# A planner fed with traced intervals, patient engines, and two blocks' operands of x made during the attention

## The chip, the cores and the metric

The kernel runs on one core of a Trainium2 chip. The metric is the device time of one execution in microseconds (us); three executions of the kernel before gave 893.12, 893.55 and 894.0, median 893.55. Engines are named as in the profile: PE (TensorE matmul), PEld (its weight load), DVE (VectorE), ACT (ScalarE), POOL (GpSimd), SP (the queue from which transfers are issued).

## The reference

```python
# B, H, S, D = 4, 8, 576, 64; window 128; x has 2304 tokens of 512, d_ff 2048
scores = scale * q @ k.T
scores = where(0 <= rel < 128, scores + slope[h] * -abs(rel), -1e9)
attn = softmax(scores)            # exp(s - max) / (sum + 1e-9)
x = attn @ v                      # heads side by side: 2304 x 512
h = x @ w_in;  x = where(h > 0, h, exp(min(h, 0)) - 1) @ w_out     # first layer (ELU)
h = x @ w2_in; x = (h * sigmoid(h)) @ w2_out                       # second layer (SiLU)
```

The two layers' weights come as 64-bit floats and are turned into 32-bit ones on the chip.

## The kernel before

**Work.** The attention has 36 units (9 pairs of 128-token groups x 4 pairs of heads). A unit is: scores on PE (`s`, L454), bias and maximum on DVE (L465), exponential on ACT (L473), inverse of the sums on DVE (L485, L486), scaling on POOL (L492), transposes on PE (`t`, L511), their eviction to `pt` by DVE and ACT (L521, L523); for every two units a product with v on PE (`a`, L543). Each product of the layers is made of three: every fp32 operand is split into a rounded part (ACT) and a remainder (DVE).

**First sweep of layer one.** While the attention runs, the tokens whose x is done (blocks of 256, then four of 512 tokens) go through the first four of the sixteen 128-wide slices of d_ff: `hidden` on PE (L587), ELU on ACT and DVE (L572, L573), `output_first` on PE (L614), into `acc`. One piece is three matmuls. These pieces fill PE between the units' own matmuls. The last block's pieces come behind the attention.

**The other sweeps.** The rest of both layers goes by 768-token blocks b = 0, 1, 2 in steps k = 0 to 14. A step's input products use seven combinations of four quarters of x (tiles `c`, matmuls L873); then come its output products (L964). Step 0 is block 0, step 1 block 1, step 2 block 2, then the order turns. `make(k)` loads x from DRAM (`xs`), forms differences on DVE (L759), rounds on ACT (L769) and takes the remainder on DVE (L734): 22 DVE and 14 ACT instructions per block. For blocks needed again, the seven `c` are stored to DRAM (`d`, L741), and later steps load them back with `reload` (L810). In the kernel before, steps 0, 1 and 2 use `make`; step 0's stands just behind the attention, since the tiles `c` lie where the attention's tiles were (`opened`).

**Order.** `Plan.run` is a list scheduler that runs while the program is built: each instruction has an engine, a cost, what it must follow, and a latest start (`late`) that comes from due times on PE's instructions. Of the instructions whose inputs are there by its clock, an engine takes the one with the smallest `late`. The result is a fixed order on each engine (and on SP); on the chip each engine runs its own order, one behind the other, waiting where it must. A unit's due time is `unit_due(u)`.

## Time and profile before

| what | value |
|---|---|
| median of three executions | 893.55 us (893.12 to 894.0) |
| the profiled execution: its time, its span | 892.67 us, 890.9 us (1.8 us lie outside the span) |
| PE busy | 867.2 us, 97% of the span, 5520 matmuls |
| DVE, ACT, POOL busy | 600.8, 503.1, 132.0 us |
| DMA | 130.98 MB, mean 147 GB/s |

How to read it: the profiled execution's 892.67 us is its span plus 1.8 us. Where a PE timeline says "x12 | 3.06 us", that is the time from the first matmul's start to the last one's modelled end; from the start of one run to the start of the next is the time a run really takes. A busy PE says only that matmuls were under way: at a lower granted clock the same matmuls are busy for longer.

### The profile page before, as it was taken

The page shows a single profiled execution, that of the slowest core. Times are in us where ns is not written, and L with a number is a line of the kernel's source. Part 1 is how long each engine was busy: PE and PEld are TensorE (multiplying, and loading weights), DVE is VectorE, ACT ScalarE, POOL GpSimd, SP SyncE. Part 2 cuts the span into 40 slices and gives each one's busy share as a digit, 9 for nine tenths or more (in the row PEclk, how much of TensorE's full clock was granted, in tenths as well). Part 3 has the DMA queues.
Part 4 walks back from the last instruction along what each step waited for, and adds up shares of the span by engine and source line. Part 5 has one row for each costly group of instructions (what it writes and reads, how often), then busy time and mean ns, then how long its engine had stood idle before and what let it go on. Part 6 is the DMA issues. An engine that isn't in the chain of part 4 may idle for free.

```text
span 890.9 us, 14913 instructions
## 1 busy us (share of the span) xinstructions
PE 867.2 (97%) x5520; PEld 774.6 (87%) x5520; DVE 600.8 (67%) x1385; ACT 503.1 (56%) x1191; POOL 132.0 (15%) x238
## 2 busy tenths in 40 slices
PE   5989999999979999999999999999999999999998
PEld 3667777777979999999999998989899998989997
DVE  6988876639988888896848878564847334634333
ACT  6877776657764747472637557465654244533331
POOL 8653433311010001110000003000101000000000
PEclk9979999999979999999999999999999999999999
DMA  9834341214947102181535567061327060126721
GB/s 312 277 99 149 108 155 55 72 61 164 336 126 283 36 24 72 71 321 46 216 128 216 212 228 268 10 248 48 118 80 286 1 249 24 72 71 213 250 104 71
DMA packets 55928, 130.98 MB, mean 147 GB/s; under 512 B 3760, under 2 KB 35760, under 8 KB 55856
## 3 DMA queue, kind: packets, MB, share of 16 engines
q1 hardware_dynamic: 55712, 129.91, 41.0%
q8 instruction: 43, 0.70, 0.3%
q14 instruction: 29, 0.24, 0.1%
q10 hardware_dynamic: 144, 0.13, 0.0%
HBM read 93.06 MB, written 36.96 MB: 146 GB/s over the span
## 4 chain that ended last, share of the span: by engine, by line
PE 89%; DVE 7%; ACT 2%; POOL 1%; issue 1%; POOLq 0%; DVEq 0%; ACTq 0%
PE m L964 38%; PE m L873 34%; PE m L614 5%; PE m L587 5%; PE a L543 3%; PE s L454 3%; PE t L511 2%; DVE c L734 1%; DVE raw L318 1%; DVE w L295 1%; DVE p L465 1%; DVE raw L320 1%; DVE t L759 0%; DVE e L572 0%; DVE e L573 0%
## 5 line engine op out<-in xcount | busy, mean ns | idle before, releaser
L964 PE MATMUL m<-w,g 128*128 128x512 f32 (+1 forms) x876 | 211.7, 387 | 0.0
L964 PEld LDWEIGHTS m<-w,g 128*128 128x128 f32 x876 | 161.6, 188 | 26.4
L964 PE MATMUL m<-g,w 128*128 128x384 f32 x864 | 165.4, 342 | 4.7 <-DVE h L886 2.8
L964 PEld LDWEIGHTS m<-g,w 128*128 128x128 f32 x864 | 154.9, 192 | 6.3 <-DVE h L886 3.1
L315 POOL TENSOR_SCALAR raw<-raw 128x512 f32<-128x512 f32 x60 | 50.8, 847 | 544.5 <-DMA raw<-in_moe_w_in_dram 233.3
L851 DVE TENSOR_TENSOR g<-e,g 128x384 fp32r<-128x384 f32 x168 | 92.6, 559 | 41.1 <-ACT e L837 39.4
L873 PE MATMUL m<-c,wd 128*128 128x384 f32 x504 | 101.4, 336 | 0.1
L873 PE MATMUL m<-c,wc 128*128 128x384 f32 x504 | 100.8, 336 | 0.0
L873 PE MATMUL m<-c,wa 128*128 128x384 f32 x504 | 99.5, 336 | 1.1 <-DVE c L734 0.6
L886 DVE TENSOR_TENSOR hs<-m,hs 128x384 f32<-128x384 f32 x84 | 46.7, 556 | 76.2 <-PE m L873 75.6
L978 DVE TENSOR_TENSOR acc<-m,acc 128x384 f32<-128x384 f32 (+2 forms) x85 | 51.4, 608 | 67.4 <-PE m L964 66.3
L882 ACT ACTIVATE hs<-m 128x384 f32<-128x384 f32 x84 | 41.2, 490 | 92.2 <-PE m L873 91.8
L873 PEld LDWEIGHTS m<-c,wa 128*128 128x128 f32 x504 | 89.1, 188 | 4.5 <-DVE acc L978 0.9
L873 PEld LDWEIGHTS m<-c,wd 128*128 128x128 f32 x504 | 89.0, 188 | 2.6 <-ACT h L882 0.4
L873 PEld LDWEIGHTS m<-c,wc 128*128 128x128 f32 x504 | 89.2, 188 | 2.2 <-DVE c L734 0.2
L492 POOL TENSOR_SCALAR p<-p,sm 128x192 f32<-128x192 f32 (+1 forms) x144 | 67.0, 484 | 97.2 <-DVE sm L486 58.7
L473 ACT ACTIVATE p<-p,neg 128x192 f32<-128x192 f32 (+1 forms) x144 | 63.0, 442 | 12.6 <-DVE neg L465 12.4
L614 PE MATMUL m<-g,w 128*128 128x512 f32 (+1 forms) x240 | 60.1, 393 | 1.3 <-DVE ex L573 1.0
L587 PE MATMUL m<-x,w 128*128 128x512 f32 (+1 forms) x240 | 58.0, 382 | 0.0
L614 PEld LDWEIGHTS m<-g,w 128*128 128x128 f32 x240 | 42.5, 198 | 13.1 <-issue 2.7
L838 ACT ACTIVATE g<-hs 128x384 fp32r<-128x384 f32 x48 | 25.2, 525 | 46.6 <-DVE hs L886 46.5
L873 PE MATMUL m<-c,wb 128*128 128x384 f32 x252 | 50.6, 336 | 0.0
(119 smaller groups left out, 1185.4 us busy)
## 6 DMA issues: line engine op xcount, KB each, us to landing
c<-d SPq DMA_DIRECT2D x49, 768.0 KB, 6.3
d<-c SPq DMA_DIRECT2D x28, 768.0 KB, 5.2
raw<-in_moe_w_in_dram SPq DMA_DIRECT2D x32, 512.0 KB, 5.3
raw<-in_moe_w_out_dram SPq DMA_DIRECT2D x28, 512.0 KB, 3.6
k<-in_k_dram SPq DMA_DIRECT2D x16, 384.0 KB, 4.6
d<-xs SPq DMA_DIRECT2D x7, 768.0 KB, 3.9
v<-in_v_dram SPq DMA_DIRECT2D x18, 256.0 KB, 2.7
xs<-xd SPq DMA_DIRECT2D x6, 768.0 KB, 4.8
```

What stands on the lines that cost most here:

```text
L315: add("POOL", 0.75, lambda: nc.gpsimd.tensor_scalar(f32(top()), f32(top()), 2.0 ** -112, 1.0, op0=ALU.mult, op1=ALU.mult), w=top_k)
L454: nc.tensor.matmul(T["s", j][x * (P // 2):(x + 1) * (P // 2), e, c0:], T["q", t % 2][rows, hp, o:o + P // 2], T["k", t % 2][rows, hp, o + ...
L473: nc.scalar.activation(dst, dst, AF.Exp, bias=T["neg", u % 5][:, i:i + 1], scale=-1.0, accum_out=T["sm", u % 5][:, e, j:j + 1])
L492: nc.gpsimd.tensor_scalar(dst, dst, T["sm", u % 5][:, e, j:j + 1], 1.0, op0=ALU.mult, op1=ALU.mult)
L587: nc.tensor.matmul(T[m][:, 0:w], a[:, cs], T["x0", b2][:, c, 0:w], start=(c == 0 and x == 0), stop=(c == NKC - 1 and x == 2))
L614: nc.tensor.matmul(T[m][:, 0:w], a[:, cs], b2[:, 0:w], start=(f == 0 and x == 0), stop=(f == FIRST_F - 1 and x == 2))
L851: add("DVE", 0.58, lambda: nc.vector.tensor_tensor(T[gk[1]], T[ek], f32(T[gk[0]]), op=ALU.subtract), r=[ek, gk[0]], w=[gk[1]])
L873: nc.tensor.matmul(T[m][:, 0:HALF], a[:, cs], x[:, j, c, :], start=(begin and c == 0 and n == 0), stop=(c == 1 and n == 2), skip_group_che ...
L882: add("ACT", 0.5, lambda: nc.scalar.activation(T[s], T[m][:, 0:HALF], AF.Copy), r=[m], w=[s])
L886: add("DVE", 0.58, lambda: nc.vector.tensor_tensor(T[s], T[m][:, 0:HALF], T[s], op=ALU.add), r=[m], w=[s])
L964: nc.tensor.matmul(T[m][:, 0:w], l, rr, start=(f == 0 and x == 0), stop=(f == n - 1 and x == 2))
L978: add("DVE", 0.2 + w / 1000.0, lambda: nc.vector.tensor_tensor(dst, T[m][:, 0:w], dst, op=ALU.add), r=[m], w=dk)
```

## The change

There are three parts.

1. **Costs.** Nearly all costs given to the planner become shorter (a 384-column DVE difference 0.57 to 0.475, a bias instruction 0.4 to 0.29, the exponential 0.6 to 0.445). The delay between engines, 0.2 for all, becomes 0.08 plus a drain time of the first engine; it is no longer counted between two instructions of one engine. A transfer's cost becomes 1.6 us and 300 GB/s (from 1.8 and 220). Units fall due every 3.2 us for the first 14, then every 5.0 (from 5.2).
2. **Patience.** ACT, DVE and POOL don't start an instruction where one that is over 3 us more urgent becomes ready before it would end; they take a shorter one or stay idle.
3. **`make_ahead(b)`**, for blocks 0 and 1: the same 22 DVE and 14 ACT instructions as in `make`, but issued during the attention, in the space of the third `acc` tile and two small tiles `st`, with stores of half a `c` (384 KB) to DRAM. Steps 0 and 1 then load their `c` back (7 loads of 768 KB each). x is stored per pair of groups instead of per block, and step 6's operands are stored in halves. `sm` and `neg` have four buffers instead of five.

```diff
-    LINK = 0.2
-    DMA_START = 1.8
-    DMA_RATE = 220.0e3
+    LINK = 0.08
+    DRAIN = {"PE": 0.2, "ACT": 0.1, "DVE": 0.08, "POOL": 0.04}
+    DMA_START = 1.6
+    PATIENT = "ACT", "DVE", "POOL"
+    GAIN = 3.0
+    DMA_RATE = 300.0e3
...
                     x = min(can, key=lambda x: (x[1].late, x[1].n))
+                    if eng in self.PATIENT:
+                        soon = [u for u in queues[eng] if now < u[0] < now + x[1].cost - 0.1 and u[1].late < x[1].late - self.GAIN]
+                        if soon:
+                            at = min(u[0] for u in soon)
+                            can = [x for x in can if now + x[1].cost <= at + 0.1]
+                            if not can:
+                                continue
+                            x = min(can, key=lambda x: (x[1].late, x[1].n))
...
-    UNIT, START = 5.2, 6.0
+    UNIT, FAST, NFAST, START = 5.0, 3.2, 14, 4.0
...
+    def make_ahead(b):
+
+        w = acc[NBIG - 1]
+        wk = lambda lo, n=HALF: acc_keys(NBIG - 1, lo, lo + n)
+        third = w[:, 6 * HALF:8 * HALF].bitcast(F32R).rearrange("p (x t) -> p x t", x=2)
+        stages = [(lambda i=i: T["st", i], [("st", i)]) for i in range(2)] + [(lambda: third, wk(6 * HALF, 2 * HALF))]
...
+        for c in range(2):
+            load(lambda c=c: nc.sync.dma_start(w[:, 0:2 * BIG].rearrange("p (i t) -> p i t", i=2), x_dram[b][:, c::2, :]),
+                 768 * 1024, r=[k for k in plan.keys(("xd",)) if k[1] == b], w=wk(0, 2 * BIG))
...
+            form(t3, b22, b12)
+            form(b12, b12, b11)
+            form(t2, b22, b12)
+            srcs = b11, b21, b22, b21, b12, t2, t3
+            for i in (1, 0, 5, 4, 6, 3, 2):
...
+                add("ACT", 0.42, lambda s=s, stage=stage: nc.scalar.activation(stage()[:, 0, :], s[0](), AF.Copy), r=s[1], w=sk)
+                add("DVE", 0.475, lambda s=s, stage=stage: nc.vector.tensor_tensor(stage()[:, 1, :], s[0](), f32(stage()[:, 0, :]),
+                                                                                 op=ALU.subtract), r=s[1], w=sk)
+                load(lambda i=i, c=c, stage=stage: nc.sync.dma_start(
...
+                if hp == NPAIR - 1 and (2 * t + 2) * P in (BIG, 2 * BIG):
+                    make_ahead(2 * t * P // BIG)
...
-        if k == FAR:
+        if k in (0, 1, FAR):
             return "load"
...
-        make(0)
+        for i in (0, 1, 5, 4, 6, 3, 2):
+            reload(0, i)
```

**POOL, at the start.** Ahead of these rows both orders make the bias tables of the heads; `biasm` is a masked copy of all of them that the ninth unit needs first, `p_127` and `p_128` are the probabilities of the first two units. Before:

```order
L426 TENSOR_SCALAR bias<-acc_78 128x192 x2
L424 TENSOR_SCALAR biasf<-acc_78 128x128 x2
L435 COPY biasm<-bias 128x1536
L436 MEMSET biasm 64x8x128
L492 TENSOR_SCALAR p_127<-p_127,sm_145 128x128
```

In the changed kernel:

```order
L442 TENSOR_SCALAR bias<-acc_78 128x192 x2
L508 TENSOR_SCALAR p_127<-p_127,sm_145 128x128
L508 TENSOR_SCALAR p_127<-p_127,sm_145 128x192
L508 TENSOR_SCALAR p_127<-p_127,sm_145 128x128
L508 TENSOR_SCALAR p_127<-p_127,sm_145 128x192
L440 TENSOR_SCALAR biasf<-acc_78 128x128 x2
L508 TENSOR_SCALAR p_128<-p_128,sm_147 128x128
```

The first unit's scaling moved ahead of the masked copy, and so did the second's; the copy stands behind both.

**SP, at the end of the attention.** `xd` is x in DRAM, `xt` its SBUF tile, `d` the stored combinations, `raw` the 64-bit weights. Before:

```order
L567 DMA xd_83<-xt_137 512x1x512
L750 DMA xs<-xd_81 128x2x768
L313 DMA raw_86<-in_moe_w_out_dram 128x1024
L313 DMA raw_87<-in_moe_w_out_dram 128x1024
L750 DMA xs<-xd_81 128x2x768
```

In the changed kernel:

```order
L581 DMA xd_83<-xt_137 512x1x256
L698 DMA d_172<-st_154 256x1x384
L864 DMA c_2735<-d_163 128x1536
L864 DMA c_2736<-d_164 128x1536
L864 DMA c_2740<-d_168 128x1536
L864 DMA c_2739<-d_167 128x1536
L864 DMA c_2741<-d_169 128x1536
L864 DMA c_2738<-d_166 128x1536
L864 DMA c_2737<-d_165 128x1536
L804 DMA xs<-xd_83 128x2x768
L329 DMA raw_86<-in_moe_w_out_dram 128x1024
L329 DMA raw_87<-in_moe_w_out_dram 128x1024
```

Two loads of x went; seven loads of finished operands and one of block 2's x now stand ahead of the output weights.

**DVE, behind the attention.** `e` and `g` belong to the last block's first sweep, `wa` to `wd` are split weights, `c` the operands of step 0. Before:

```order
L600 TENSOR_TENSOR g_106<-e_96,g_97 128x512
L759 TENSOR_TENSOR t_2648<-xs 128x384
L759 TENSOR_TENSOR xs<-xs 128x384
L759 TENSOR_TENSOR t_2647<-xs 128x384
L572 TENSOR_SCALAR e_96<-e_96 128x512
L573 TENSOR_TENSOR e_96<-m_158,e_96 128x512
L734 TENSOR_TENSOR c_2633<-xs,c_2633 128x384
```

In the changed kernel:

```order
L613 TENSOR_TENSOR g_106<-e_96,g_103 128x512
L311 TENSOR_TENSOR wd_2726<-raw_87,wd_2725 128x512
L585 TENSOR_SCALAR e_96<-e_96 128x512
L586 TENSOR_TENSOR e_96<-m_158,e_96 128x512
L311 TENSOR_TENSOR wa_2728<-raw_84,wa_2727 128x512
L613 TENSOR_TENSOR g_112<-e_96,g_109 128x512
```

The rows of step 0's operands are gone from this place; only the last block's ELU and the splits of step 0's input weights are left.

## Rows read from the trace of the kernel before

**Rows 1.** Windows: us; busy PE, PEld, DVE, ACT, POOL; PEclk, DMA share, GB/s.

```profile
0.00:24.00 24.00, 15.07 (x168) 9.59 (x170) 15.24 (x72) 15.89 (x55) 19.56 (x50) 1.00 0.94 318
24.00:60.00 36.00, 31.05 (x352) 23.29 (x355) 32.81 (x107) 28.96 (x90) 24.12 (x39) 0.86 0.60 198
60.00:196.00 136.00, 135.75 (x1404) 98.57 (x1397) 95.52 (x350) 97.89 (x303) 45.83 (x101) 1.00 0.30 94
196.00:222.00 26.00, 25.02 (x109) 19.89 (x108) 21.25 (x39) 17.75 (x37) 2.02 (x3) 1.00 0.52 173
222.00:252.90 30.90, 30.90 (x176) 30.39 (x176) 28.84 (x55) 23.23 (x50) 5.26 (x6) 1.00 0.76 279
252.90:269.30 16.40, 11.81 (x44) 10.86 (x44) 13.94 (x28) 9.79 (x20) 1.47 (x2) 0.69 0.41 131
269.30:524.00 254.70, 254.70 (x1459) 254.70 (x1458) 203.59 (x401) 142.39 (x295) 15.10 (x19) 1.00 0.40 149
524.00:542.50 18.50, 17.83 (x93) 15.78 (x92) 13.70 (x25) 12.44 (x28) 3.06 (x4) 1.00 0.74 260
542.50:887.60 345.10, 345.09 (x1735) 311.51 (x1734) 175.48 (x313) 154.80 (x324) 15.59 (x17) 1.00 0.36 131
```

**Rows 2.** PE's waits, 0 to 200 us: total us, times, longest.

```profile
PE t L511 <- POOL p L492: 3.2, 5, 1.0
PE s L454 <- DVE neg L465: 3.1, 3, 1.3
PE t L511 <- ACT pt L523: 2.9, 2, 2.6
```

**Rows 3.** Timeline of POOL from 8 us: start, us, what.

```profile
8.22 1.46 POOL L435 COPY biasm<-bias 128x1536 bf16<-128x1536 bf16 x1
...
10.79 3.02 POOL L492 TENSOR_SCALAR p<-p,sm 128x128 f32<-128x128 f32 x8
```

**Rows 4.** Timeline of PE, 60 to 292 us.

```profile
73.64 3.06 PE L587 MATMUL m<-x,w 128*128 128x512 f32 x12
76.62 0.77 PE L454 MATMUL s<-k,q 64*64 64x192 f32 x16
...
198.88 9.68 PE L587 MATMUL m<-x,w 128*128 128x512 f32 x42
208.40 8.81 PE L614 MATMUL m<-g,w 128*128 128x512 f32 x37
```

**Rows 5.** The same, where step 0 starts and ends.

```profile
221.85 2.70 PE L873 MATMUL m<-c,wa 128*128 128x384 f32 x14 [0.61 <-DVE c L734]
...
246.54 6.41 PE L964 MATMUL m<-g,w 128*128 128x384 f32 x36
255.72 2.08 PE L964 MATMUL m<-g,w 128*128 128x384 f32 x6 [2.77 <-DVE h L886]
...
260.30 9.07 PE L964 MATMUL m<-g,w 128*128 128x384 f32 x35 [1.16 <-DVE g L851]
269.21 2.27 PE L873 MATMUL m<-c,wa 128*128 128x384 f32 x12
```

**Rows 6.** Chain that ended last, 190 to 300 us.

```profile
213.52 1.41 DVE c L734 x3
```

**Rows 7.** Groups by form: count, busy us, mean ns.

```profile
L769 ACT ACTIVATE c<-xs 128x384 fp32r<-128x384 f32 x30 | 14.7, 517 | 2.8 <-DVE xs L759 1.4 <-PE m L873 1.3
```

**Rows 8.** DMA issues: count, KB each, median us to landing.

```profile
c<-d SPq DMA_DIRECT2D x49, 768.0 KB, 6.3
...
xd<-xt SPq DMA_DIRECT2D x3, 512.0 KB, 4.4
```

**Rows 9.** Windows for line 492 alone: POOL's busy us and its instructions.

```profile
0.00:20.00 20.00, 5.44 (x14) 1.00 0.93 305
20.00:40.00 20.00, 9.98 (x19) 1.00 0.95 328
...
60.00:100.00 40.00, 14.80 (x34) 1.00 0.38 120
```

More of the change, by code (lines that the diff above doesn't have):

```diff
@@ L64, in keys, with between @@
         return [k for k in set(self.writer) | set(self.readers) if k[0] in names]
+    def between(self, a, b):
+        return a.tail + self.LINK if a.eng != b.eng or a.moved else 0.0
     def run(self):
         for op in reversed(self.ops):
-            op.late = min([op.due] + [b.late - self.LINK - op.cost - op.tail for b in op.before])
+            op.late = min([op.due] + [b.late - op.cost - self.between(op, b) for b in op.before])
         waiting = {op: len(op.after) for op in self.ops}
@@ L101, in run @@
                         if not waiting[b]:
-                            at = max(a.end + (self.LINK if a.eng != b.eng else 0.0) for a in b.after)
+                            at = max(a.end + (self.between(a, b) if not a.moved else self.LINK) for a in b.after)
                             queues.setdefault(b.eng, []).append((at, b))
@@ L235, in attention_elu_silu_kernel @@
         fixed(att_p, ("pt", i), [P, 2, 4 * P], F32)
-    for i in range(5):
+    for i in range(4):
         fixed(att_p, ("neg", i), [P, 4], F32)
@@ L441, in unit_due @@
     def unit_due(u):
[L442 removed]
+        return START + min(u, NFAST) * FAST + max(u - NFAST, 0) * UNIT
     def scores(u):
@@ L481, in normal @@
         t, hp = UNITS[u]
-        sm = [("sm", u % 5, i) for i in range(4)]
+        sm = [("sm", u % 4, i) for i in range(4)]
         def invert():
-            nc.vector.tensor_scalar_add(T["sm", u % 5], T["sm", u % 5], 1.0e-9)
-            nc.vector.reciprocal(T["sm", u % 5], T["sm", u % 5])
-        add("DVE", 0.36, invert, w=sm)
+            nc.vector.tensor_scalar_add(T["sm", u % 4], T["sm", u % 4], 1.0e-9)
+            nc.vector.reciprocal(T["sm", u % 4], T["sm", u % 4])
+        add("DVE", 0.3, invert, w=sm)
         for j in range(2):
@@ L555, in split_x, with store_x @@
         xk = [("xt", bi % 2, c, i) for i in range(w // (2 * P))]
-        cost = 0.16 + w / 1000.0
-        add("ACT", cost, lambda: nc.scalar.activation(T["x0", 0][:, c, 0:w], src(), AF.Copy), r=xk, w=[("x0", 0, c)])
+        cost = 0.1 + w / 1000.0
+        add("ACT", cost - 0.08, lambda: nc.scalar.activation(T["x0", 0][:, c, 0:w], src(), AF.Copy), r=xk, w=[("x0", 0, c)])
         add("DVE", cost, lambda: nc.vector.tensor_tensor(T["x0", 1][:, c, 0:w], src(), f32(T["x0", 0][:, c, 0:w]), op=ALU.subtract),
             r=xk + [("x0", 0, c)], w=[("x0", 1, c)])
-    def store_x(bi):
-        g0, n = blocks[bi]
-        o = 0
-        while o < n * P:
-            b, i = divmod(g0 * P + o, BIG)
-            w = min(n * P - o, BIG - i)
-            load(lambda b=b, i=i, w=w, o=o: nc.sync.dma_start(x_dram[b][:, :, i:i + w], T["xt", bi % 2][:, :, o:o + w]),
-                 NKC * w * P * 4, r=[("xt", bi % 2, c, h) for c in range(NKC) for h in range(n // 2)], w=[("xd", b, bi)])
-            o += w
+    def store_x(t):
+        bi, o = home[2 * t]
+        b, i = divmod(2 * t * P, BIG)
+        w = 2 * P
+        load(lambda: nc.sync.dma_start(x_dram[b][:, :, i:i + w], T["xt", bi % 2][:, :, o:o + w]),
+             NKC * w * P * 4, r=[("xt", bi % 2, c, o // w) for c in range(NKC)], w=[("xd", b, t)])
     def elu(src, e):
@@ L635, in emit @@
             if f == FIRST_F - 1:
-                add("ACT", 0.1 + w / 1000.0 + 0.16 * (w == 4 * P and g0 * P // BIG != (g0 * P + w - 1) // BIG), keep, r=[m], w=ak)
+                add("ACT", 0.06 + w / 1200.0 + 0.1 * (w == 4 * P and g0 * P // BIG != (g0 * P + w - 1) // BIG), keep, r=[m], w=ak)
         return emit
@@ L741, in store_combo, with store_lanes @@
         load(lambda: nc.sync.dma_start(d, f32(x().rearrange("p x c t -> p (x c t)"))), 768 * 1024, r=r, w=[("d", layer, b, i)])
+    def store_lanes(layer, b, i, x, r):
+        d = scratch[layer, b, i] = dram_p.tile([P, 4 * HALF], F32, tag=f"d{layer}{b}{i}", name=f"d{layer}{b}{i}")
+        for c in range(2):
+            load(lambda c=c: nc.sync.dma_start(d.rearrange("p (x c t) -> p x c t", x=2, c=2)[:, :, c, :], f32(x()[:, :, c, :])),
+                 384 * 1024, r=r(c), w=[("d", layer, b, i, c)])
     def make(k):
@@ L750, in make @@
                 load(lambda c=c: nc.sync.dma_start(T["xs",], x_dram[b][:, c::2, :]), 768 * 1024,
-                     r=plan.keys(("xd",)), w=[("xs", i, j) for i in range(2) for j in range(2)])
+                     r=[x for x in plan.keys(("xd",)) if x[1] == b], w=[("xs", i, j) for i in range(2) for j in range(2)])
             else:
@@ L791, in place @@
             for c in range(2):
-                add("ACT", 0.5, lambda c=c: nc.scalar.activation(stage()[:, 0, c, :], s[c][0](), AF.Copy), r=s[c][1],
+                add("ACT", 0.42, lambda c=c: nc.scalar.activation(stage()[:, 0, c, :], s[c][0](), AF.Copy), r=s[c][1],
                     w=[("xs", 0, c)])
-                add("DVE", 0.57, lambda c=c: lower_half(stage(), c, s[c][0]()), r=s[c][1] + [("xs", 0, c)], w=[("xs", 1, c)])
-            store_combo(layer, b, i, stage, [("xs", x, c) for x in range(2) for c in range(2)])
+                add("DVE", 0.475, lambda c=c: lower_half(stage(), c, s[c][0]()), r=s[c][1] + [("xs", 0, c)], w=[("xs", 1, c)])
+            store_lanes(layer, b, i, stage, lambda c: [("xs", x, c) for x in range(2)])
         form(temp, b22, b12)
@@ L810, in reload @@
         load(lambda: nc.sync.dma_start(f32(T["c", i].rearrange("p x c t -> p (x c t)")), scratch[layer, b, i]), 768 * 1024,
-             r=[("d", layer, b, i)], w=c_keys(i))
+             r=[("d", layer, b, i)] + [("d", layer, b, i, c) for c in range(2)], w=c_keys(i))
     def source(k):
```

108 lines of the change are left out of this document (61 added, 47 removed).

## The prediction

> **What bounds the kernel now.** I first cut the span into windows at the places where PE's timeline changes its look [rows 1]. From 269.3 to 524 and from 542.5 to 887.6 PE is busy without a gap at the full clock (PEclk 1.00): 600 of the 890.9 us are PE's own work, and an order that keeps it fed gains nothing there. What PE loses lies in four places. From 0 to 24 us it is idle for 8.9 us, from 24 to 60 for 5.0 us at a mean clock of 0.86; from 196 to 222 it is idle for 1.0 us; and from 252.9 to 269.3 for 4.6 us with the clock at 0.69. Between 524 and 542.5 it is idle for 0.7 us.
>
> For the start I then read PE's waits: three chains, POOL's scaling, DVE's maxima, the eviction on ACT, hold it for 9.2 us in all [rows 2]. From 24 to 60 DVE is busy for 32.8 of 36 us: there DVE sets the pace, with the first blocks' weights to convert beside the units. From 60 to 196 it is the other way round: PE has 0.25 us of idle time, DVE 40.5, ACT 38.1 [rows 1].
>
> Where step 0's outputs should run, the timeline shows three waits for DVE and ACT [rows 5], and DVE is at 28.8 of 30.9 us in the window before [rows 1]. The run of 36 matmuls at 246.54 takes 6.41 us, so one takes 0.178 us at full clock. From its end at 252.95 to 269.21 there are 42 matmuls (6, 1 and 35), 7.5 us of work in 16.3 us: 8.8 us are lost, 4.6 of them as idle time and the rest because the run of 35 takes 9.07 us, that is 0.259 us each. PE fell to its lower level behind its own idle time. DVE is full there because it makes the operands of steps 0 and 1 beside the activations and the weights.
>
> **The change part by part.** *Operands off the transition.* Steps 0 and 1 lose 44 DVE and 28 ACT instructions between 196 and 269 us. The chain has three of the DVE ones in 1.41 us [rows 6], 0.47 us each, 20.7 us in all. An ACT one has 0.517 us [rows 7], 14.5 us in all at most. In the window up to 252.9 DVE has 2.1 us of slack, so what DVE owes at 252.9 (PE's 4.6 us of idle time, and the clock behind it) is far less than the 20.7 us taken away. But something takes its place: in SP's new order seven loads of `c` and one of x stand ahead of the output weights. Seven loads of 768 KB are 5.5 MB; at the 279 GB/s of the window from 222 to 252.9 [rows 1] that is 20 us. The first can't start before x's last tile has been written out, some 5 us behind the last attention product (4.4 us to landing, rows of the same kind [rows 8]), and takes 6.3 us to land [rows 8]. PE has the last block's first sweep to do meanwhile: 105 matmuls of 512 columns, at 9.52 us for 42 [rows 4] 23.8 us. So the first `c` has 12 us to spare, and the last, which the seventh product needs, lands about as it is wanted. The output weights, however, are now converted during step 0: DVE's order has 57 instructions there, of about half a microsecond each, in the 31 us that PE took before from step 0's first product to its stall. I take back 6.0 of the 8.8 us (bounds 2 and 8.8), and the whole 1.0 us before 222, which was a wait for an operand now loaded [rows 5].
>
> *The start.* The scaling of the first unit stood behind the masked copy that POOL begins at 8.22 us; it began at 10.79 us, 2.57 us later [rows 3]. In the new order it stands ahead. I take 2.5 us. The bounds are 0, since DVE's work up to the fourteenth unit is instruction for instruction the same and it is busy for 32.8 of 36 us, and 9.2 us, all three chains.
>
> *Coarser pieces.* I counted in PE's two orders the runs of first-sweep matmuls between the units' own: 51 before, 33 after, and 14 fewer among those of 512 columns. A run of 12 takes 2.98 us from its start to the next one's [rows 4]; 12 at the pace of the unbroken run of 42 (0.227 us each) would be 2.72 us. Each break costs 0.26 us, 14 fewer give 3.6 us (bounds 0 and 3.6).
>
> *Operands into the attention.* The same 44 and 28 instructions come to lie between 60 and 200 us. DVE's load there rises from 95.5 to 116 of 136 us, 85%; ACT's from 97.9 to 112, 83%. PE stays the slowest, if the order keeps its chains short; patience is meant for that, and its idle time on DVE comes out of the 20 us left. The near ends are the windows themselves: at 70% DVE load PE loses 0.25 us of 136, at 91% (24 to 60 us) 5.0 of 36. A straight line between them would give 13 us at 85%. But from 222 to 252.9 DVE is at 93% and PE loses nothing, because PE has work in hand [rows 1], as it has here: every unit has a run of 12 beside it in the new order. I take a loss of 3 us (bounds 0 and 13). The stores of half a `c` are 28 of 384 KB, 10.8 MB, where the DMA engines are 30% busy [rows 1]; each ACT rounding into a small tile waits for the store three before it, and with 28 of them in some 100 us the three before take over 10, so I charge nothing for that. If the cover fails, what is late is the next exponential behind it on ACT.
>
> *The rest.* Block 0's and block 1's stores leave the transition, their loads come: 14 loads of 768 KB, in a stretch with DMA time to spare. The planner's shorter costs move output pieces in the later steps; with PE fed without a gap [rows 1] I charge nothing, bounds 1.5 us either way: the window from 524 to 542.5 could give back its 0.7 us of idle time, or another place lose as much.
>
> **The sum** is 2.5 + 3.6 + 1.0 + 6.0 - 3.0 = 10.1 us. It comes off the profiled execution's 892.67 us: 882.6. The median of the runs before lies 0.9 us above that execution, so the forecast for the median is 883.5 us.
>
> **The rivals.** *All of it arrives.* The transition gives back 8.8 us, the start 5, the layer boundary 1.5, and the attention loses nothing: 8.8 + 1.0 + 5 + 3.6 + 1.5 = 19.9, 873.5 us. For it speaks that DVE is relieved by more than it owed; against it the 91% of DVE at the start.
>
> *The transition's wait is replaced by one for the output weights*, which now queue on SP behind the operands and, on DVE, fall into step 0. Then 6.0 us stay lost: 889.5 us. Against it: DVE is busy for 21.3 of 26 us while the last block's sweep runs [rows 1], and step 0's operands, up to 10.3 us of it (22 x 0.47), are gone from there.
>
> *POOL's scaling is slowed by DVE's added differences.* One scaling takes 0.389 us before 20 us, 0.525 from 20 to 40, and 0.435 from 60 to 100 us [rows 9]. The second window is the one in which DVE converts weights from two SBUF operands. If the attention goes back to 0.525 us, a unit's four scalings take 0.36 us longer, 7.9 us over 22 units if each held PE up: 891.4 us. POOL's total can't be the cause, at 45.8 of 136 us [rows 1]. The Trainium skill has this as a rule (SBUF — State Buffer, section Who interferes with whom): a DVE instruction with two SBUF inputs contends with a GpSimd instruction that reads SBUF, and the one that comes second waits. By that rule, which the three windows agree with, the added differences are of just this kind.
>
> *The attention becomes DVE's and ACT's* (the other side). The 20.7 us of DVE work are not hidden: each unit waits for an instruction that isn't its own. Its place is the units from about the seventeenth on. The gains without the charge are 13.1 us, so it decides from the point where 13.1 of the 20.7 us are not hidden; with all of it PE is 20.7 us later, 893.55 + 20.7 - 13.1 = 901 us. For it speaks the straight line above, against it the 40.5 us of idle DVE time and the runs of 12.
>
> **How the numbers follow.** About 0.2% (1.8 us) is what a measurement of this kernel can tell from no change. Chances: the forecast (878 to 888) 0.50; all of it 0.18; the transition's wait replaced 0.12; POOL slowed 0.08; the attention bound by DVE and ACT 0.12. The first three are faster, and POOL's case is split about the bound of 891.8 us: faster 0.82, same 0.06, slower 0.12. The range is 873 to 893 us: below it lies a part of the second case, above it most of the last.
>
> **What would show it.** The windows again: behind the attention DVE well under 90% busy and no PE wait over 1 us up to step 1; PE waits to 20 us shorter by 2 to 3 us; the first-sweep runs in twelves; in the attention PE idle for no more than 3 us and DVE near 85%. The forecast is wrong if PE's clock drops between 60 and 200 us, if `t` waits for POOL there, or if an output product of step 0 waits for weights that landed late.

## The result and the profile after

The changed kernel takes 878.27 us (median of four executions, 877.71 to 879.3); before took 893.77 us beside it. The ratio is 0.983 [0.981, 0.985], a gain of 15.5 us where 10 were forecast. The profiled execution took 878.51 us, with a span of 876.7 us.

First the windows of the changed kernel, cut where its PE timeline changes its look (columns as in [rows 1]).

```profile
0.00:24.00 24.00, 15.91 (x174) 9.78 (x175) 15.42 (x76) 15.87 (x57) 19.52 (x50) 1.00 0.95 316
24.00:60.00 36.00, 30.55 (x348) 23.42 (x348) 33.11 (x102) 29.92 (x90) 23.54 (x40) 0.86 0.66 215
60.00:196.00 136.00, 135.07 (x1414) 101.48 (x1404) 117.29 (x396) 110.47 (x332) 52.61 (x100) 1.00 0.61 198
196.00:217.00 21.00, 21.00 (x95) 17.37 (x94) 11.61 (x21) 10.81 (x20) 0.00 (x0) 1.00 0.89 350
217.00:252.00 35.00, 35.00 (x202) 34.79 (x201) 30.82 (x58) 25.41 (x50) 5.60 (x8) 1.00 0.70 267
252.00:270.00 18.00, 18.00 (x104) 18.00 (x103) 17.11 (x34) 8.41 (x18) 1.83 (x3) 1.00 0.17 55
270.00:524.00 254.00, 253.34 (x1445) 252.21 (x1445) 201.45 (x385) 148.91 (x304) 19.78 (x23) 1.00 0.39 140
524.00:873.30 349.30, 349.30 (x1758) 315.68 (x1757) 175.87 (x317) 157.23 (x327) 13.36 (x17) 1.00 0.36 132
```

In these two profiles the start has hardly changed: PE is idle for 8.1 us up to 24 us, where it was 8.9, and from 24 to 60 its busy time and its clock are nearly the same [rows 1]. In the attention DVE's 95.5 us have become 117.3 of 136 us (86%), and PE's idle time only went from 0.25 to 0.93 us (0.52 of it is one wait at 190.21). From 196 to 270 us PE isn't idle at all and its clock stays at 1.00, even where DVE is at 17.1 of 18 us.

The same place in PE's timeline (start, us, what; the wait before a run in brackets). L600 and L627 are the first sweep's products, L927 and L1018 the input and output products that were L873 and L964 in [rows 5].

```profile
190.21 0.97 PE L627 MATMUL m<-g,w 128*128 128x512 f32 x3 [0.52 <-ACT acc L635]
...
193.00 2.34 PE L627 MATMUL m<-g,w 128*128 128x512 f32 x9
195.17 11.04 PE L600 MATMUL m<-x,w 128*128 128x512 f32 x48
206.05 11.05 PE L627 MATMUL m<-g,w 128*128 128x512 f32 x48
216.94 2.24 PE L927 MATMUL m<-c,wa 128*128 128x384 f32 x12
...
241.98 9.72 PE L1018 MATMUL m<-g,w 128*128 128x384 f32 x54
251.54 1.22 PE L927 MATMUL m<-c,wa 128*128 128x384 f32 x6
...
271.36 3.41 PE L1018 MATMUL m<-g,w 128*128 128x384 f32 x18 [0.66 <-DVE e L898]
```

Step 0 starts 3.3 us earlier (216.94 for 220.22) and no longer waits for an operand. Its outputs run as 54 matmuls without a gap, 9.56 us to the next run's start or 0.177 us each: the pace at full clock that [rows 5] show only ahead of the stall. The one wait behind the attention is 0.66 us, in step 1.

PE's waits over the whole span (total us, times, longest):

```profile
PE t L527 <- ACT pt L539: 5.0, 4, 1.5
PE s L470 <- DVE bias L437: 3.7, 1, 3.7
PE s L470 <- DVE neg L481: 2.1, 3, 1.1
...
PE t L527 <- POOL p L508: 0.3, 1, 0.3
```

The wait for POOL's scaling fell from 3.2 to 0.3 us, but that for the eviction on ACT rose from 2.9 to 5.0 [rows 2]. (The 3.7 us for the bias table, ahead of the first scores, were there before.)

To see where the time came from I cut both spans at two events: the first 512-column piece, which ends the start, and step 0's first input product.

| stretch | before, us | after, us | gain, us | forecast, us |
|---|---|---|---|---|
| to the first 512-column piece | 70.70 | 70.09 | 0.6 | 2.5 |
| from there to step 0's first product | 149.52 | 146.85 | 2.7 | 3.6 - 3.0 |
| from there to the end of the span | 670.7 | 659.8 | 10.9 | 1.0 + 6.0 |
| span | 890.9 | 876.7 | 14.2 | 10.1 |

The first row is less certain than it looks. e1 and e12 below run before's order on all four engines, unchanged, up to that piece, and reach it at 72.37 and 72.56 us instead of 70.70. What differs first in them is PE's granted clock, from 20 to 28 us: 1.00 before and in the changed kernel, 0.57 in e1 and in e12. In e12:

```profile
20.00:28.00 8.00, 6.49 (x54) 4.56 (x54) 5.89 (x25) 5.75 (x21) 5.51 (x10) 0.57 1.05 380
```

The changed kernel's start, profiled four times (here and in e2, e3 and e6, which don't touch it), ends at 69.04 to 70.16 us with no such drop. So the start gained 0.6 us by this pair and 2.3 to 2.5 us against e1 and e12; which of the two is typical isn't shown.

The last stretch splits further when the n-th matmul behind step 0's first is compared in both. At the 300th the changed kernel is 10.2 us ahead (the transition); it loses 1.0 of them around the wait in step 1 and is 8.9 to 9.2 us ahead up to the 1680th. By the 1860th, where the layers meet, it is 10.7 us ahead, and stays so (the end of the span adds 0.2). The medians differ by 1.3 us more than the two spans, mainly because the profiled execution of before lies 1.1 us below its median.

### The profile page after: what moved, and what is told of

Its sections match the earlier page's. It is cut to its first block, busy times and chain, and to the rows that moved or that the text cites. A ratio compares the mean times of both kernels' runs of the same rounds, so it can differ in the third digit from the quotient of the medians.

```text
span 876.7 us, 15017 instructions
## 1 busy us (share of the span) xinstructions
PE 858.5 (98%) x5520; PEld 772.8 (88%) x5520; DVE 603.1 (69%) x1385; ACT 507.0 (58%) x1191; POOL 136.2 (16%) x238
## 4 chain that ended last, share of the span: by engine, by line
PE 89%; DVE 7%; ACT 2%; DMA 1%; issue 1%; POOL 0%; SPq 0%; POOLq 0%; DVEq 0%; ACTq 0%
PE m L1018 37%; PE m L927 33%; PE m L600 5%; PE m L627 5%; PE a L559 3%; PE s L470 3%; PE t L527 2%; DVE raw L334 1%; DVE p L481 1%; DVE raw L336 1%; DVE pt L537 1%; ACT p L489 1%; DVE w L311 1%; DVE g L905 0%; DMA q<-in_q_dram 0%
## 5 line engine op out<-in xcount | busy, mean ns | idle before, releaser
L1018 PE MATMUL m<-w,g 128*128 128x512 f32 (+1 forms) x876 | 211.9, 387 | 0.0
L1018 PEld LDWEIGHTS m<-w,g 128*128 128x128 f32 x876 | 161.6, 188 | 26.2
L1018 PE MATMUL m<-g,w 128*128 128x384 f32 x864 | 162.1, 336 | 0.7 <-DVE e L898 0.7
L1018 PEld LDWEIGHTS m<-g,w 128*128 128x128 f32 x864 | 151.6, 188 | 1.5 <-DVE e L898 1.2
L331 POOL TENSOR_SCALAR raw<-raw 128x512 f32<-128x512 f32 x60 | 47.5, 792 | 539.3 <-DMA raw<-in_moe_w_in_dram 258.3
L927 PE MATMUL m<-c,wd 128*128 128x384 f32 x504 | 101.3, 335 | 0.0
L927 PE MATMUL m<-c,wc 128*128 128x384 f32 x504 | 101.2, 335 | 0.0
L927 PE MATMUL m<-c,wa 128*128 128x384 f32 x504 | 98.9, 336 | 0.0
L927 PEld LDWEIGHTS m<-c,wa 128*128 128x128 f32 x504 | 89.2, 188 | 2.6
L927 PEld LDWEIGHTS m<-c,wc 128*128 128x128 f32 x504 | 89.2, 188 | 2.1
L927 PEld LDWEIGHTS m<-c,wd 128*128 128x128 f32 x504 | 89.1, 188 | 2.0
L508 POOL TENSOR_SCALAR p<-p,sm 128x192 f32<-128x192 f32 (+1 forms) x144 | 74.5, 534 | 83.8 <-DVE sm L502 37.9
L627 PE MATMUL m<-g,w 128*128 128x512 f32 (+1 forms) x240 | 57.2, 388 | 1.3 <-DVE e L586 0.7
L600 PE MATMUL m<-x,w 128*128 128x512 f32 (+1 forms) x240 | 55.3, 377 | 1.2 <-DVE x L574 1.2
L627 PEld LDWEIGHTS m<-g,w 128*128 128x128 f32 x240 | 42.9, 198 | 11.4 <-issue 1.3
L927 PE MATMUL m<-c,wb 128*128 128x384 f32 x252 | 50.7, 335 | 0.0
```

Of the source, the lines that this page charges most:

```text
L331: add("POOL", 0.66, lambda: nc.gpsimd.tensor_scalar(f32(top()), f32(top()), 2.0 ** -112, 1.0, op0=ALU.mult, op1=ALU.mult), w=top_k)
L508: nc.gpsimd.tensor_scalar(dst, dst, T["sm", u % 4][:, e, j:j + 1], 1.0, op0=ALU.mult, op1=ALU.mult)
L600: nc.tensor.matmul(T[m][:, 0:w], a[:, cs], T["x0", b2][:, c, 0:w], start=(c == 0 and x == 0), stop=(c == NKC - 1 and x == 2))
L627: nc.tensor.matmul(T[m][:, 0:w], a[:, cs], b2[:, 0:w], start=(f == 0 and x == 0), stop=(f == FIRST_F - 1 and x == 2))
L927: nc.tensor.matmul(T[m][:, 0:HALF], a[:, cs], x[:, j, c, :], start=(begin and c == 0 and n == 0), stop=(c == 1 and n == 2), skip_group_che ...
L1018: nc.tensor.matmul(T[m][:, 0:w], l, rr, start=(f == 0 and x == 0), stop=(f == n - 1 and x == 2))
```

## The experiments

Four questions were open. Did the transition need all of the 20.7 us taken off DVE, or much less, and does the planner alone cure it? Does POOL's order or DVE's work pace the start? How much more DVE work does the attention hide? And which of the planner's edits makes the order good? These are the milestones of the kernels that answer them, with the ratio of their time to that of before.

| kernel | median, us | ratio [95%] | first 512-col. piece | step 0's first product | stretch between | PE's waits over 0.15 us in it | 512-col. runs in it | from there to the end |
|---|---|---|---|---|---|---|---|---|
| before | 893.77 | | 70.70 | 220.22 | 149.52 | 0.37 | 39 | 670.7 |
| after | 878.27 | 0.983 [0.981, 0.985] | 70.09 | 216.94 | 146.85 | 0.52 | 25 | 659.8 |
| e1 | 890.22 | 0.995 [0.993, 0.997] | 72.37 | 225.42 | 153.05 | 3.70 | 38 | 662.8 |
| e2 | 883.93 | 0.988 [0.986, 0.991] | 70.14 | 216.47 | 146.33 | 0 | 25 | 666.0 |
| e3 | 879.21 | 0.983 [0.980, 0.986] | 70.16 | 216.21 | 146.05 | 0 | 25 | 661.1 |
| e4 | 895.66 | 1.002 [1.000, 1.003] | 72.62 | 222.25 | 149.63 | 0.37 | 39 | 671.7 |
| e5 | 869.54 | 0.973 [0.971, 0.976] | 61.12 | 207.12 | 146.00 | 0.26 | 25 | 660.1 |
| e6 | 889.59 | 0.996 [0.995, 0.998] | 69.04 | 228.06 | 159.02 | 7.79 | 25 | 659.7 |
| e7 | 882.92 | 0.989 [0.985, 0.992] | 70.94 | 218.15 | 147.21 | 1.22 | 25 | 661.0 |
| e8 | 881.80 | 0.987 [0.985, 0.989] | 70.98 | 220.01 | 149.03 | 0 | 43 | 660.8 |
| e9 | 890.73 | 0.996 [0.994, 0.998] | 71.11 | 217.54 | 146.43 | 0.37 | 27 | 668.6 |
| e10 | 881.51 | 0.986 [0.985, 0.988] | 69.96 | 221.69 | 151.73 | 4.50 | 26 | 658.8 |
| e11 | 880.01 | 0.984 [0.983, 0.986] | 72.09 | 217.92 | 145.83 | 0.32 | 25 | 660.3 |
| e12 | 891.21 | 0.998 [0.997, 0.999] | 72.56 | 222.21 | 149.65 | 0.37 | 39 | 667.9 |

The milestones come from one profiled execution each. The time of the first 512-column piece differs by 1.9 us between executions of one and the same order (70.70 and 72.56, see above), so a difference of 2 us there, in one execution, says little.

### The two halves of the change

**e1: operands ahead, old planner.** The kernel before with `make_ahead`, the loads and the stores of the change (x per pair of groups, step 6's operands in halves) and its four buffers, at the planner's old costs, delays and due times.

```diff
+    def make_ahead(b):
...
+                if hp == NPAIR - 1 and (2 * t + 2) * P in (BIG, 2 * BIG):
+                    make_ahead(2 * t * P // BIG)
...
-        make(0)
+        for i in (0, 1, 5, 4, 6, 3, 2):
+            reload(0, i)
```

> Operands of steps 0 and 1 made during the attention, with the old planner (its costs, delays, due times, no patience). Theory A, the gain is the transition: the stall behind 252.9 us is gone, some 10 of the 15.5 us come, 882 to 885 us. Theory B, the gain is the planner's: the added 20.7 us of DVE work find no place in the old order, PE waits in the attention, the time is 888 us or more.

**e2: new planner, operands as before.** The changed kernel without `make_ahead`; the stores in halves and the four buffers stay.

```diff
-                if hp == NPAIR - 1 and (2 * t + 2) * P in (BIG, 2 * BIG):
-                    make_ahead(2 * t * P // BIG)
...
-        if k in (0, 1, FAR):
+        if k == FAR:
...
-        for i in (0, 1, 5, 4, 6, 3, 2):
-            reload(0, i)
+        make(0)
```

> New costs, due times and patience, but steps 0 and 1 make their operands behind the attention as before. Theory A: the stall at step 0's outputs stays, only the coarser pieces and the start count, 888 to 892 us. Theory B: the new order hides the operands' DVE work too and PE's loss at step 0 is under 3 us, 880 to 884 us.

e1 gained 3.5 us, e2 9.8 us, together less than the whole change's 15.5, though both also carry the side edit that e12 tests alone. Behind step 0 the two halves add up: at the 1500th matmul they are 6.0 and 2.8 us ahead, the whole change 9.0. It is in the attention that they need each other. There e1 loses 3.70 us to new waits and keeps its 38 short runs, so its time is the one that theory B named, although the stretch behind step 0 is 7.9 us shorter, as theory A had it. Three of the waits, in e1's PE timeline:

```profile
194.54 0.34 PE L513 MATMUL t<-ident,p 64*128 64x64 f32 x4 [0.75 <-POOL p L494]
...
204.70 8.46 PE L586 MATMUL m<-x,w 128*128 128x512 f32 x36 [1.65 <-ACT acc L621]
...
217.33 8.26 PE L613 MATMUL m<-g,w 128*128 128x512 f32 x35 [0.53 <-DVE g L599]
```

e2's time lies in the range of its theory B, but not for B's reason alone: the attention loses nothing, the stretch behind step 0 is 4.7 us shorter (1.7 of it where the layers meet, as in e1), and the stall is still there in a smaller form, now at the output weights:

```profile
247.47 0.61 PE L1016 MATMUL m<-g,w 128*128 128x384 f32 x2 [1.96 <-ACT w L308]
248.69 5.02 PE L1016 MATMUL m<-g,w 128*128 128x384 f32 x26 [0.61 <-DVE w L311]
```

So the charge for the attention (3 us in the forecast) is real with the old planner and about half a microsecond with the new one.

**e3: one block ahead.** Only block 0's operands are made during the attention.

```diff
-                if hp == NPAIR - 1 and (2 * t + 2) * P in (BIG, 2 * BIG):
+                if hp == NPAIR - 1 and (2 * t + 2) * P == BIG:
...
-        if k in (0, 1, FAR):
+        if k in (0, FAR):
```

> As the changed kernel, but only block 0's operands are made ahead; step 1 makes its own during step 0. Theory A1, it is step 1's operands that collide with step 0's outputs: nearly the whole loss at step 0's outputs comes back, 885 to 887 us. Theory A2, DVE owed only a few us and either block relieves it: 878 to 881 us.

879.21 us can't be told from the whole change, as theory A2 had it. The second block gives 1.3 us behind step 0 (661.1 against 659.8) and costs 0.8 in the attention. What DVE owed at the stall was a few microseconds, and with the new planner half of the 20.7 us taken off covers it.

### The start

**e4: masked copies late, on the kernel before.** Both copies may not start before 13 us by the planner's clock, so the first units' scalings stand ahead of them.

```diff
-        add("POOL", 2.9, lambda: cut("biasm", slice(P // 2, P), slice(0, P)), r=every, w=[("biasm", h) for h in range(H)])
+        add("POOL", 2.9, lambda: cut("biasm", slice(P // 2, P), slice(0, P)), r=every, w=[("biasm", h) for h in range(H)], floor=13.0)
```

> The kernel before, with the two masked copies of the bias kept back on POOL until the first two units are scaled; nothing else is changed on purpose. The prediction's term: 2.5 us faster, about 891. Rival: the start is paced by DVE's work up to the fourteenth unit, the earlier scaling is lost again by 60 us, within 1 us of before.

POOL's timeline in e4 shows the order that was wanted:

```profile
8.63 1.52 POOL L492 TENSOR_SCALAR p<-p,sm 128x128 f32<-128x128 f32 x4 [0.46 <-DVE sm L486]
...
12.96 1.46 POOL L435 COPY biasm<-bias 128x1536 bf16<-128x1536 bf16 x1
```

The first scaling starts 2.16 us earlier than in [rows 3]. The time is 895.66 us: not better, if anything 1.3 us worse by the ratio (a little outside the rival's 1 us), and the first 512-column piece comes at 72.62 us, as in e1 and e12. Why the 2.16 us aren't there is seen in PE's timeline of the kernel before, and, below it, of the changed kernel:

```profile
8.70 1.82 PE L454 MATMUL s<-k,q 64*64 64x128 f32 x16 [1.05 <-DVE neg L465]
11.22 1.62 PE L511 MATMUL t<-ident,p 64*128 64x64 f32 x12 [0.69 <-POOL p L492]
```

```profile
8.75 1.83 PE L470 MATMUL s<-k,q 64*64 64x128 f32 x16 [1.05 <-DVE neg L481]
10.51 0.90 PE L527 MATMUL t<-ident,p 64*128 64x64 f32 x12
12.69 0.90 PE L527 MATMUL t<-ident,p 64*128 64x64 f32 x12 [1.27 <-ACT pt L539]
```

PE had scores to do until 10.5 us anyway, so POOL's lateness had cost 0.69 us, not 2.57. And what the first transposes gain, the second ones lose to the eviction.

**e5: less DVE work at the start.** The two DVE instructions that merge the bits of each of the first sweep's weight tiles are left out, so those weights, and with them the output, aren't the reference's.

```diff
-        add("DVE", 0.61, lambda: nc.vector.scalar_tensor_tensor(low(), top(), 0x80000000, low(), op0=ALU.bitwise_and,
-                                                               op1=ALU.bitwise_or), r=top_k, w=low_k)
-        add("DVE", 0.61, lambda: nc.vector.scalar_tensor_tensor(top(), top(), 3, low(), op0=ALU.logical_shift_left,
-                                                               op1=ALU.bitwise_or), r=low_k, w=top_k)
+        if not (layer == 0 and f < FIRST_F):
...
```

> The changed kernel without the two DVE instructions that put together the high and low words of the first eight weight tiles (16 instructions of 0.6 to 1.0 us in the first 60 us), so the first sweep computes with wrong weights. If DVE's work paces the start, the first 512-column piece, at 70.1 us now, starts 8 to 12 us earlier and the time falls to 867 to 871. If the chains of single units pace it (scores, maxima, exponentials, scaling, transposes), it starts less than 4 us earlier and the time stays above 874.

The window from 24 to 60 us of e5, and its first 512-column piece in PE's timeline:

```profile
24.00:60.00 36.00, 33.71 (x469) 26.81 (x462) 29.73 (x119) 33.24 (x109) 21.43 (x42) 1.00 0.57 185
```

```profile
61.12 0.86 PE L601 MATMUL m<-x,w 128*128 128x512 f32 x3
```

The piece comes 9.0 us earlier, PE does 469 matmuls in the window instead of 348, at full clock where the changed kernel has 0.86, and 8.7 us of it arrive at the end. So part of the 9.0 us is the clock's. DVE's work is what sets the pace of the start, by its load or as a link in each weight tile's own chain: e5 lightens both at once, and no run parts them.

**e11: some of it on POOL.** The remainders of the four output-weight tiles of the first sweep go from DVE to POOL, nothing is left out.

```diff
-            split_weight(tag, None, top, None, 4 * P, top_k, "DVE")
+            split_weight(tag, None, top, None, 4 * P, top_k, "POOL" if kind else "DVE")
```

> The changed kernel with the remainders of the first sweep's four output-weight tiles computed by POOL instead of DVE. If DVE's work is what sets the pace before 70 us, as the run without the merges of the first weights says, the 2 us or so taken off DVE move the first 512-column piece forward by 1 to 2.5 us, and the time is 876 to 877.5. Rival: POOL, which has the masked copy and the scaling there, becomes late and the transposes wait for it: the first piece is no earlier, 878 to 881.

The rival was right: the time, 880.01 us, is no better, and the transposes do wait for POOL. (That the first piece is 2.0 us later isn't all the edit's: at 46 us, where the orders of DVE and POOL first differ, e11 is already 0.7 to 0.8 us late, with a granted clock of 0.79 from 20 to 28 us.) DVE isn't relieved, since some of its other instructions become longer. In e11, of POOL's, DVE's and PE's timelines:

```profile
46.57 1.67 POOL L311 TENSOR_TENSOR w<-acc,w 128x512 fp32r<-128x512 f32 x1 [2.06 <-ACT w L308]
...
47.01 1.78 DVE L334 SCALAR_TENSOR_TENSOR acc<-acc 128x512 uint32<-128x512 uint32 x1
...
49.26 1.63 POOL L508 TENSOR_SCALAR p<-p,sm 128x192 f32<-128x192 f32 x4 [1.01 <-DVE sm L502]
...
49.81 1.61 PE L527 MATMUL t<-ident,p 64*128 64x64 f32 x16 [3.23 <-POOL p L508]
```

A merge (L334) beside POOL's first remainder takes 1.78 us; the sums' inverse stands behind it on DVE, the scaling waits for that, and PE waits 3.23 us for the scaling. In the changed kernel the same merge, with POOL on its scaling:

```profile
47.08 0.69 DVE L334 SCALAR_TENSOR_TENSOR acc<-acc 128x512 uint32<-128x512 uint32 x1
```

Over the four merges from 24 to 60 us of this kind the mean is 1070 instead of 766 ns, and 1.78 us is the longest of them. That e11 shows no gain is measured, and so is the chain of waits; that POOL's new work is what lengthens the merge is read from their overlap, and no run here removed it alone.

### The attention

**e6: most of the added DVE work twice.** 36 of the 44 DVE instructions of `make_ahead` are issued a second time with the same result, 16.9 us more.

```diff
             form(t3, b22, b12)
+            form(t3, b22, b12)
...
-                add("DVE", 0.475, lambda s=s, stage=stage: nc.vector.tensor_tensor(stage()[:, 1, :], s[0](), f32(stage()[:, 0, :]),
-                                                                                 op=ALU.subtract), r=s[1], w=sk)
+                for _ in range(2):
+                    add("DVE", 0.475, lambda s=s, stage=stage: nc.vector.tensor_tensor(stage()[:, 1, :], s[0](), f32(stage()[:, 0, :]),
+                                                                                     op=ALU.subtract), r=s[1], w=sk)
```

> The changed kernel with 36 of the 44 DVE instructions in the operands made ahead issued twice (16.9 us more DVE work in the attention; the result is the same). If DVE's idle time covers them, 878 to 881 us with DVE over 93% busy from 70 to 190 us. If 85% was already near the edge, PE waits there by 8 us or more and the time is 886 to 895.

The time is 11 us longer than the changed kernel's, and all of that comes between the first 512-column piece and step 0 (159.02 for 146.85 us). A window of e6 at the end of the attention, and two of the waits in it:

```profile
160.00:207.00 47.00, 40.84 (x331) 29.49 (x326) 39.29 (x103) 27.28 (x72) 11.58 (x20) 0.93 0.56 181
```

```profile
178.16 0.73 PE L627 MATMUL m<-g,w 128*128 128x512 f32 x2 [1.47 <-DVE g L613]
...
193.03 0.34 PE L527 MATMUL t<-ident,p 64*128 64x64 f32 x4 [1.92 <-POOL p L508]
```

PE is idle for 6.2 of these 47 us (3.6 of them waiting for POOL's scaling, 2.5 for DVE itself), and its mean granted clock falls to 0.93, so the loss is larger than the waits. The changed kernel's 86% DVE load is hidden almost whole, and the next 17 us are hidden to a third: the edge is close.

**e7: no patience.** An engine takes the most urgent instruction that is ready, as before.

```diff
-    PATIENT = "ACT", "DVE", "POOL"
+    PATIENT = ()
```

> The changed kernel without patience: an engine takes the most urgent of what is ready. If patience keeps the units' chains short under the added work, PE waits in the attention and the time is 882 us or more. If the runs of 12 beside each unit cover late chains anyway, 877 to 880 us.

882.92 us (880.91 to 885.98): without patience 4.6 us are lost by the medians, 2.4 by the profiled spans. In that profiled execution they are spread over all three stretches (0.9, 0.4 and 1.2 us), so no one place of it is shown.

**e8 and e9: due times.** e8 is the changed kernel with the old due times; e9 the kernel before with the new ones and nothing else.

```diff
     def unit_due(u):
-        return START + min(u, NFAST) * FAST + max(u - NFAST, 0) * UNIT
+        return 6.0 + 5.2 * u
```

> The changed kernel with the old due times of the units (every 5.2 us from 6.0 on). If due times at 3.2 us push the first units forward, the first 512-column piece starts 2 us or more later and the time is 880 or more; if DVE's work paces the start whatever the order, 877 to 880 us.

```diff
-    UNIT, START = 5.2, 6.0
+    UNIT, FAST, NFAST, START = 5.0, 3.2, 14, 4.0
...
-        return START + u * UNIT
+        return START + min(u, NFAST) * FAST + max(u - NFAST, 0) * UNIT
```

> The kernel before with nothing changed but the units' due times (every 3.2 us for the first 14 units, then every 5.0, start at 4.0 instead of 5.2 and 6.0); every cost is still the old one, and no operand is made ahead. If the due times alone gather PE's 512-column pieces into longer runs, the runs between the first piece and step 0 number about 25 instead of 39, that stretch is 2 to 3 us shorter than the 149.5 us of before, and the time is 890.5 to 892. Rival: the due times do so only together with the shorter costs; then there are still 35 to 45 runs and the time is within 1.5 us of 893.8, on either side.

The due times make the long runs, whatever the costs: 43 runs in e8, 27 in e9, 39 before. e8's time, 881.80 us, is the one that its first theory gave, but the place is another: the first piece is only 0.9 us later, and 2.2 us are lost in the stretch behind it. e9's stretch is 3.1 us shorter than before's with 12 fewer breaks and the same waits: 0.26 us for each, the forecast's price. Between before and after, waits taken off, it is 2.8 us for 14 breaks, 0.20 us each, and between the changed kernel and e8 2.7 us for 18, 0.15 us each. So the count of breaks gives the size only roughly. The stall at step 0's outputs is untouched in e9:

```profile
252.13 1.31 PE L964 MATMUL m<-g,w 128*128 128x384 f32 x6 [2.51 <-DVE h L886]
...
254.87 0.69 PE L964 MATMUL m<-g,w 128*128 128x384 f32 x1 [1.43 <-ACT g L850]
...
256.72 7.95 PE L964 MATMUL m<-g,w 128*128 128x384 f32 x35 [1.16 <-DVE g L851]
```

**e10: old instruction costs.** All instruction costs are again those of before; delays, transfers, due times and patience stay new.

```diff
-                add("DVE", 0.29, biased, r=[("s", j), (b, 2 * hp + j)], w=pk[:1] + [("neg", u % 4, i)])
+                add("DVE", 0.4, biased, r=[("s", j), (b, 2 * hp + j)], w=pk[:1] + [("neg", u % 4, i)])
...
-                add("DVE", 0.475, lambda: nc.vector.tensor_tensor(d[0](), x[0](), y[0](), op=ALU.subtract), r=x[1] + y[1], w=d[1])
+                add("DVE", 0.57, lambda: nc.vector.tensor_tensor(d[0](), x[0](), y[0](), op=ALU.subtract), r=x[1] + y[1], w=d[1])
```

> The changed kernel with all instruction costs as they were before (the delay between engines, the transfers, the due times, the patience and the operands made ahead stay). If the traced intervals are what makes the planner place DVE's added work well, the longer costs bring back part of the 3.7 us of PE's idle time that the operands made ahead had under the old planner, and short waits behind step 0: 881 to 886 us. Rival: the instruction costs matter little beside the delay, the due times and the patience; then 877 to 880.

881.51 us, 3.2 us more. The attention's waits are back at 4.50 us (0.52 in the changed kernel); the short waits that were expected behind step 0 didn't come (658.8 us). The traced intervals matter where DVE is nearly full.

### Where the layers meet

**e12: one side edit.** The kernel before, with the operands of step 6, the first of layer two, stored in halves.

```diff
-            store_combo(layer, b, i, stage, [("xs", x, c) for x in range(2) for c in range(2)])
+            store_lanes(layer, b, i, stage, lambda c: [("xs", x, c) for x in range(2)])
```

> The kernel before with one side edit of the change alone: the operands of step 6, the first of layer two, are stored to DRAM in halves of 384 KB instead of whole. Both kernels that carried half of the change, and the whole one, gained 1.2 to 1.5 us against before between the 1680th and the 1860th matmul behind step 0's first, where the layers meet; the kernel with the due times alone, which lacks this edit, gained nothing there. If the halves are the cause, this kernel gains 1.0 to 1.5 us at that place and nothing elsewhere: 892.2 to 892.9 us. Rival: the gain there comes from another part that the two halves share (the store of x per pair of groups, or the tiles' places); then the waits of 0.15 and 0.47 us near 526 and 533 us stay and the time is within 0.7 us of 893.8.

The gain between the 1560th and the 1860th matmul behind step 0's first is 1.8 us (0.9 to 2.7 us ahead of before), more than the 1.0 to 1.5 expected. Before, PE waited there:

```profile
526.46 3.41 PE L964 MATMUL m<-g,w 128*128 128x384 f32 x18 [0.15 <-ACT e L837]
...
533.09 1.34 PE L873 MATMUL m<-c,wa 128*128 128x384 f32 x6 [0.47 <-DVE acc L978]
```

The place where PE waited for 0.15 us, in e12's timeline:

```profile
522.05 3.31 PE L970 MATMUL m<-g,w 128*128 128x384 f32 x18
525.20 1.23 PE L879 MATMUL m<-c,wd 128*128 128x384 f32 x6
```

The waits of before are gone, and so is PE's idle time of 0.7 us in the window from 524 to 542.5 [rows 1]. A store in halves frees half the staging tile earlier, and the planner orders the work around it anew; the two can't be told apart here. This edit, for which the forecast had only its 1.5 us either way, gave 1.8 us, and the changed kernel is 1.7 us further ahead over the same matmuls. The median gained 2.3 us. The 0.9 us by which e12 is ahead of before already at the transition aren't the edit's: up to 434 us all four engines run before's order. PE's mean granted clock is 0.83 in the 20 us from 254.2 on in e12, 0.74 in the same 20 us of before, from 252.2 on: the place varies by so much between executions.

## Why the prediction was right, and where it was off

The sign, the main mechanism (DVE relieved behind the attention) and the range (873 to 893 us) held; 883.5 us was 5.2 us too high, and 878.27 lies at the lower end of the band that the forecast gave itself (878 to 888). In the order of the sum:

- **The start, 2.5 us: the failed step.** The step took POOL's delay of 2.57 us for PE's. PE's row at 8.70 us, on which the step did not draw, shows that it had scores until 10.5 us and lost 0.69 us to POOL. e4 moved the scaling and gained nothing, e5 took DVE work away and gained 9.0 us: what the prediction gave as the reason for its lower bound of 0, DVE's load, is what sets the pace. The start came to 0.6 us in the profiled pair. Against e1 and e12 it came to 2.3 to 2.5 us, but they run before's own order, POOL's too, and what differs is the granted clock; if theirs is the usual start, the step's size was luck.
- **Coarser pieces, 3.6 us: mis-sized.** 2.8 us came; the runs put a break at 0.15 to 0.26 us, and the step took 0.26. e8 and e9 show that the due times alone make the runs.
- **The transition, 1.0 + 6.0 us: right, mis-sized.** 10.2 us came by the 300th matmul, all that was lost there, and 9.2 are left behind step 1's wait. I held 2.8 us back for the output weights, which queue behind the operands and are converted during step 0. They were in time: DVE did its 58 instructions there in 30.8 of 35 us, and the 54 outputs at 241.98 us ran without a gap. In e2, where DVE still makes the operands, PE waits 1.96 us for such weights, and in e1, with the old planner, 0.71 and 0.42 us at step 0's outputs: the rival of the output weights is real for either half alone. e1 and e2 show that both halves reach the stall, by 6.0 and 3.4 us at the 300th matmul.
- **The attention, -3.0 us: mis-sized.** PE's waits between the first 512-column piece and step 0 rose by 0.15 us. The charge is right for the old planner (e1: 3.70 us of waits) and for the old costs (e10: 4.50), and wrong for the order that the new numbers make. Of the two near ends that were weighed, the window with work in hand was the better guide, not the straight line.
- **The rest, 0 +- 1.5 us.** 1.7 us came at the place that was named, from the stores in halves (1.8 in e12), a little over the bound.

The rival with the opposite sign is refuted for this load and shown for the next one: 16.9 us more cost 11 us (e6). POOL's scaling did become slower, but only in part through DVE's added differences. The scaling alone (POOL's busy us and instructions in windows: L508 in the changed kernel and, without operands made ahead, in e2; L492 before):

The changed kernel:

```profile
60.00:100.00 40.00, 17.18 (x34) 1.00 0.56 178
...
140.00:196.00 56.00, 19.59 (x36) 1.00 0.54 179
```

e2, and then before:

```profile
60.00:100.00 40.00, 17.72 (x34) 1.00 0.43 134
...
140.00:196.00 56.00, 16.67 (x35) 1.00 0.15 49
```

```profile
140.00:196.00 56.00, 15.97 (x36) 1.00 0.12 39
```

From 60 to 100 us one takes 0.505 us, where [rows 9] gave 0.435; but e2, with no difference added, has 0.521, so there it is the new order and not the added work. From 140 to 196 one takes 0.444 us before, 0.476 in e2 and 0.544 in the changed kernel: there the added differences show. ([rows 9] also mix two widths: half of the scalings before 20 us are the narrower ones, 128x128, and from 20 to 40 us nearly all are 128x192, so the prediction's step from 0.389 to 0.525 us isn't all slowing.) PE waited 0.3 us for POOL in the whole span, so the slowing was real and off the path. In e6, with more such work on DVE, PE waits 3.6 us for POOL behind 70 us. The Trainium skill's rule (SBUF — State Buffer, section Who interferes with whom), by which a DVE instruction with two SBUF inputs and a GpSimd instruction that reads SBUF contend, agrees with the rows from 140 to 196 us and with e11's merge of 1.78 us.

Of the signs that were named, two were wrong: the waits to 20 us did not shrink by 2 to 3 us (PE was idle for 7.5 us there before and for 7.1 after), and DVE was not well under 90% behind the attention (17.1 of 18 us from 252 to 270). PE didn't wait there all the same. The others came: runs of twelve (twelve matmuls at 73.11 us and often after), DVE at 86%, PE idle for under 3 us. (One sum is off: by its own terms the rival in which all of it arrives comes to 873.7 us, not 873.5. Nothing hangs on it.)

Left open: what the start gained, 0.6 or some 2.4 us, and why the clock stayed up in it; the place of the 2.4 to 4.6 us that patience is worth; and whether a version faster than this one lies in the start; e5 says that up to 9 us would come from less DVE work there, e11 that POOL isn't where these remainders can go.

## What to carry to other kernels

A late instruction costs only what its reader waits: before pricing a delay on one engine, look up what the waiting engine was doing in that time. What an engine owes at a stall can be far less than what is taken off it (one block did nearly as much as two), and the same work put elsewhere is free only up to an edge, so measure the distance to it by doing the added work twice. A scheduler's due times and costs are a change of their own: run each alone, and small side edits too. And before a milestone of one execution is read, look for a second execution of the same order: here two of them differed by 1.9 us.

## What the runs showed of the hardware

- Going between small attention matmuls and runs of 512 columns cost PE 0.15 to 0.26 us per run by three pairs of kernels, with no idle time shown.
- With DVE at 95% for 18 us (252 to 270) PE was never idle; with DVE at 84% for 47 us (e6) it was idle for 6.2 us, waiting for DVE and for POOL's scaling: the load alone doesn't tell.
- One merge on DVE took 1.78 us beside a 1.67 us remainder on POOL (e11), and 0.69 us in the changed kernel; from 140 to 196 us POOL's scaling took 0.476 us in e2, and 0.544 us with DVE's added differences beside it.
- The same order on all engines reached the same matmul at 70.70 and at 72.56 us (before and e12), with a granted clock of 1.00 and 0.57 from 20 to 28 us.
